# An mLSTM cell followed by a GELU block: the short rests of four pairs of hidden tiles in one TensorE section

## The chip, the cores and the metric

The kernel runs on one core of one Trainium2 chip. The metric is device time in microseconds (us) of one execution, the median of three runs. The engines are TensorE (PE in the profile, with its weight loads PEld), VectorE (DVE), ScalarE (ACT), GpSimd (POOL) and SyncE (SP), which issues most DMAs.

## The reference

An mLSTM cell runs over batch 4, 8 heads, 768 steps and head dimension 40. Its output, gated, is laid out as 3072 tokens of 320 values and goes through a two-layer block:

```
h = x @ w_in                               # x [3072, 320], w_in [320, 2048]
g = h * (1.0 / (1.0 + np.exp(-1.702 * h)))
return (g @ w_out).astype(np.float32)      # w_out [2048, 320]
```

Everything is fp32. The change concerns `x @ w_in`, the first product.

## The kernel before, in words

The 768 steps are cut into six blocks of 128 (w = 0 to 5; NW is 6). A block has 512 tokens: 128 steps of each of the 4 batches. For every block the first product is computed, then the second, and into the instructions of the second the cell of the next block is woven. The order on every engine is the order in which the instructions are written (`manual_schedule`, line 68); the framework inserts the waits and gives each new PSUM tile one of the banks of its pool.

**The first product.** The 2048 hidden columns are 8 pairs (j = 0 to 7) of two 128-column tiles. Block 0 is done plainly (`up`, line 614). Blocks 1 to 5 use `up_fast` (line 692): of the 320 input rows, the first 256 are a 2 by 2 scheme of 128-row parts and token halves, done with seven products of 128x128 by 128x256 instead of eight. The seven operands on the token side are sums made on VectorE in `token_sums` (line 673). The results of a pair are two rows of 512 tokens: row 0 (written to `g[:, 0]`) and row 1 (`g[:, 1]`). Product 1 is needed by itself, products 5 and 6 by themselves, products 2 and 3 add up in the bank of row 0, products 4 and 7 in that of row 1.

**The rests.** The last 64 of the 320 input rows are "the rest" of a row. A rest matmul has only 64 rows, so two of them, one for row 0 on partitions 0 to 63 and one for row 1 on partitions 64 to 127, run side by side in TensorE (line 717). They add into the same banks as products 2, 3, 4, 7. In an even pair they come last and in the odd pair after it first, so that those of two pairs stand together: four sections in a block, and twenty in blocks 1 to 5. In block 4 (`w == NW - 2`) each rest is cut into two halves of 256 tokens.

The profile records every fp32 matmul as two instructions, called passes here: the 280 calls of line 709 (5 blocks, 8 pairs, 7 products) are 560 records.

**The banks.** PSUM has eight banks. The pool `ps_m` (line 67) gives single banks, four of them; `ps_a` (line 66) gives two tiles of two banks. A pair takes two single banks (product 1; row 0) and one double tile `both` (row 1; products 5 and 6). A new tile has to wait until the last reader of an earlier tile in the same bank is done.

**Out of the banks.** After the matmuls of a pair ScalarE copies product 1 to `y` (line 743). VectorE adds product 6 to it (`u2`, line 746), then adds `u2` to product 5 and to the right half of row 1 in one instruction (line 747), and then makes `g[:, 1]` from row 1 (line 750). Row 0 is copied by ScalarE (line 754) and completed by GpSimd (line 755), but in pairs 6 and 7 VectorE does it in one instruction (line 757). The GELU of pair j-1 (`gelu_fast`, two ScalarE instructions, `g[:, 1]` first) stands in pair j between the copy of product 1 and that of row 0; that of pair 7 follows the loop (line 950).

**Beside it on VectorE.** Before pair 0, in blocks 1 to 4, VectorE does `token_sums` and then `gates(w + 1)` (lines 929 to 931), a chain of small instructions for the next block that ends in lines 325 and 326. After pairs 2 to 6 it does block transposes (`block_transposes`, line 394) for the next block: after pair 6 two of them, for n = 5 and 7 (line 942). Block 5 has no next block and none of this.

**The second product.** `down_fast` (line 805) follows at once. Each of its products runs over eight hidden tiles, two passes each. The first reads `g` of pairs 0 to 3, the second `g` of pairs 4 to 7 (line 810), so its seventh tile is `g[:, 0]` of pair 7.

Of the kernel before, what the change touches and what calls it, by code (L numbers as in the profile page):

```python
# [8 lines left out]
FP = mybir.dt.float32  # L9
# [3 lines left out]
OP = mybir.AluOpType  # L13
# [13 lines left out]
def kernel(  # L27
# [17 lines left out]
    NW = S // L  # L45
    NP = H // 2
    NF = DFF // 128
    D1 = D + 1
    DP = 64
    W = B * L  # L50
# [13 lines left out]
    op = ctx.enter_context(tc.tile_pool(name="op", bufs=2))  # L64
    rows = ctx.enter_context(tc.tile_pool(name="rows", bufs=2, space=bass.MemoryType.DRAM))
    ps_a = ctx.enter_context(tc.tile_pool(name="ps_a", bufs=2, space=PSUM))
    ps_m = ctx.enter_context(tc.tile_pool(name="ps_m", bufs=4, space=PSUM))
    ctx.enter_context(tc.manual_schedule())

    V, A, G, T = nc.vector, nc.scalar, nc.gpsimd, nc.tensor  # L70
# [15 lines left out]
    w_in_x = const.tile([128, NF // 2, 128], FP, name="w_in_x")  # L86
# [140 lines left out]
    kT, qT, ys, xT, gs, o_ps, sums, vw, x_row = {}, {}, {}, {}, {}, {}, {}, {}, {}  # L227
# [109 lines left out]
    def banks(name):  # L337
        return ps_a.tile([128, 2, 512], FP, tag="a", name=name)
# [322 lines left out]
    half_w = W // 2  # L661
    temps, second = {}, {}
# [25 lines left out]
    def gelu_fast(w, j):  # L688
        for i in (1, 0):
            A.activation(out=gs[w, j][:, i, :], in_=gs[w, j][:, i, :], func=AF.Gelu_apprx_sigmoid)  # L690

    def up_fast(w, j):

        x, rest_x = temps[w], xT[w].rearrange("p c b t -> p c (b t)")
        late = j % 2 == 0
        p1, row0 = (ps_m.tile([128, W], FP, tag="m", name="p_h") for _ in range(2))
        both = banks("p_h")  # L700
        row1 = both[:, 0, :]
        flat = both.rearrange("p i t -> p (i t)")
        left, right = slice(0, half_w), slice(half_w, W)
        f = lambda c, i: w_in_sb[:, c, (2 * j + i) * 128:(2 * j + i + 1) * 128]

        def product(n, out, start, stop):
            a = {1: lambda: f(0, 0), 2: lambda: f(1, 0), 3: lambda: s_in[:, 2, j], 4: lambda: f(1, 1),
                 5: lambda: s_in[:, 0, j], 6: lambda: s_in[:, 1, j], 7: lambda: f(0, 1)}[n]()
            T.matmul(out, a, x[n], start=start, stop=stop)  # L709

        def rest():
            n = 2 if w == NW - 2 else 1
            for h in range(n):
                t = slice(h * W // n, (h + 1) * W // n)
                for i, row in enumerate((row0, row1)):
                    r = slice(i * 64, i * 64 + 64)
                    T.matmul(row[:, t], w_in_x[r, j, :], rest_x[r, 2, t], start=(not late and h == 0),  # L717
                             stop=(late and h == n - 1))

        def row_0():  # L720
            product(2, row0[:, left], late, False)
            product(3, row0[:, right], False, not late)

        def row_1():
            product(4, row1[:, left], late, False)
            product(7, row1[:, right], False, not late)

        if not late:
            rest()
        product(1, p1[:, left], True, True)  # L730
        if late:
            row_0()
        product(5, both[:, 1, left], True, True)
        product(6, both[:, 1, right], True, True)
        row_1()
        if late:
            rest()
        else:
            row_0()
        y = work.tile([L, 2, DM + 64], FP, tag="y", name="parts").rearrange("p a b -> p (a b)")  # L740
        u2 = second[w]
        g = gs[w, j] = gp.tile([128, 2, W], FP, tag="g", name="g")
        A.copy(out=y[:, left], in_=p1[:, left])  # L743
        if j:
            gelu_fast(w, j - 1)
        V.tensor_tensor(out=u2, in0=both[:, 1, right], in1=y[:, left], op=OP.add)  # L746
        V.tensor_tensor(out=y[:, half_w:3 * half_w].rearrange("p (a t) -> p a t", a=2),  # L747
                        in0=flat[:, half_w:3 * half_w].rearrange("p (a t) -> p a t", a=2),
                        in1=u2.unsqueeze(1).to_broadcast([128, 2, half_w]), op=OP.add)
        V.tensor_tensor(out=g[:, 1, :], in0=row1, in1=y[:, half_w:3 * half_w], op=OP.add)  # L750
        u = y.rearrange("p (a t) -> p a t", t=half_w)[:, 0:3:2]
        g0 = g[:, 0, :].rearrange("p (a t) -> p a t", a=2)
        if j < NF // 2 - 2:
            A.copy(out=g[:, 0, :], in_=row0)  # L754
            G.tensor_tensor(out=g0, in0=g0, in1=u, op=OP.add)  # L755
        else:
            V.tensor_tensor(out=g0, in0=row0.rearrange("p (a t) -> p a t", a=2), in1=u, op=OP.add)
# [145 lines left out]
    for w in range(NW):  # L903
# [24 lines left out]
        else:  # L928
# [4 lines left out]
            for j in range(NF // 2):  # L933
                up_fast(w, j)
                if w == 1 and j < 4:
                    weight_sums(j)
                if more and j == 2:
                    load(w + 1, "vk")
                    columns_in(w + 1)
                    spread(w + 1)  # L940
                if more and j:
                    for n in ((), (0, 2), (4,), (6, 1), (3,), (5, 7), ())[j - 1]:
                        block_transposes(w + 1, n)
                if more and j == 7:
                    columns_turn(w + 1)
                if 2 <= j < 6:
                    hidden_difference(w, j - 2)
                if j >= 6:
                    hidden_sums(w, (j - 6,), G)
# [54 lines left out]
```

## Time and profile before

| | |
|---|---|
| median of 3 runs | 466.91 us (466.19 to 467.08) |
| the profiled execution | 466.95 us; its span in the trace 465.2 us |
| TensorE busy | 459.8 us, 99% of the span, 5063 matmul records |
| VectorE, ScalarE, GpSimd busy | 340.3, 189.5, 163.5 us |
| line 709, the seven products | 240 + 160 + 80 + 80 records, 66.9 + 41.1 + 23.9 + 23.8 us |
| line 717, the rests of blocks 1 to 5 | 128 records of 64x512 and 64 of 64x256, 31.8 + 8.0 us |
| block 2, first product | 182.5 to 215.0 us of the span |

Times in views of the trace are us from the start of the span, then the duration in us; a line of the timeline may merge several instructions (x4). Busy times of matmuls overlap, since a pass starts before the one ahead of it has left the array: what a pass costs is read from the distance of starts.

### The profile page before, as it was taken

The numbers are of one execution on the slowest core, as the hardware profiler recorded it, in microseconds if no ns is written. First come the engines' busy times: TensorE is split into PE (matmuls) and PEld (weight loads), VectorE is DVE, ScalarE is ACT, GpSimd is POOL, SyncE is SP. The second block draws the span as 40 slices with busy tenths as digits, with TensorE's granted clock in tenths as the row PEclk, the third lists the DMA queues.
The fourth block names the chain that finished last, engine by engine and source line by source line (L and its number), as shares of the span: only waits on it lengthen the run. The fifth ranks groups of instructions, "written<-read, shape, count | busy, mean of one in ns | idle before, by whom it ended". The sixth has DMA issues, their size and how long they took to land.

```text
span 465.2 us, 12360 instructions
## 1 busy us (share of the span) xinstructions
PE 459.8 (99%) x5063; PEld 387.8 (83%) x5063; DVE 340.3 (73%) x698; ACT 189.5 (41%) x433; POOL 163.5 (35%) x153
## 2 busy tenths in 40 slices
PE   8999999999999999999999999999999999999996
PEld 6877877776769999778999678999878999777996
DVE  5788999699779777688875688876768867535622
ACT  5686779001546500654700554900454810354100
POOL 5101318000898600365700266700248510157000
PEclk9999999999999999999999999999999999999999
DMA  8999998049993045996034988024999306000000
GB/s 165 186 306 234 242 220 179 3 105 188 143 153 97 18 98 122 182 140 132 3 72 126 193 133 156 12 58 99 195 140 106 90 19 140 28 1 0 1 29 30
DMA packets 135561, 52.87 MB, mean 114 GB/s; under 512 B 101984, under 2 KB 131632, under 8 KB 135504
## 3 DMA queue, kind: packets, MB, share of 16 engines
q1 hardware_dynamic: 127136, 50.27, 55.5%
q10 hardware_dynamic: 8048, 1.66, 1.8%
q8 instruction: 40, 0.66, 0.6%
q0 software_dynamic: 320, 0.15, 0.2%
q14 instruction: 17, 0.14, 0.1%
HBM read 44.52 MB, written 7.54 MB: 112 GB/s over the span
## 4 chain that ended last, share of the span: by engine, by line
PE 88%; POOL 4%; DMA 3%; DVE 2%; issue 1%; ACT 0%; SPq 0%; DVEq 0%; POOLq 0%
PE p_out L818 33%; PE p_h L709 21%; PE p_h L717 7%; PE p_h L626 6%; PE p_out L764 6%; PE p_c L602 3%; DMA q_sq<-in_q_dram 2%; PE p_o L503 2%; PE p_s L459 2%; PE p_i L511 2%; PE p_h L635 2%; PE p_t L386 1%; POOL g L755 1%; PE p_s L448 1%; POOL g L786 1%
## 5 line engine op out<-in xcount | busy, mean ns | idle before, releaser
L755 POOL TENSOR_TENSOR g<-g,parts 128x512 f32<-128x512 f32 x30 | 38.2, 1274 | 191.7 <-DVE parts L747 184.3
L743 ACT COPY parts<-p_h 128x256 f32<-128x256 f32 x40 | 14.9, 373 | 152.0 <-PE p_h L709 149.2
L818 PE MATMUL p_out<-w_out_sb,g 128*128 128x160 f32 x480 | 69.6, 301 | 0.1
L818 PEld LDWEIGHTS p_out<-w_out_sb,g 128*128 128x128 f32 x480 | 66.5, 190 | 1.2 <-ACT g L690 0.4
L709 PE MATMUL p_h<-xT,w_in_sb 128*128 128x256 f32 x240 | 66.9, 388 | 0.0
L690 ACT ACTIVATE g<-g 128x512 f32<-128x512 f32 x80 | 50.1, 631 | 40.0 <-DVE g L750 24.3
L709 PEld LDWEIGHTS p_h<-xT,w_in_sb 128*128 128x128 f32 x240 | 43.7, 190 | 18.5 <-issue 7.5
L823 DVE TENSOR_TENSOR o_sb<-o_sb,p_out 128x160 f32<-128x160 f32 x70 | 21.4, 317 | 41.0 <-PE p_out L818 40.4
L818 PE MATMUL p_out<-t_sb,s 128*128 128x160 f32 x320 | 47.1, 300 | 0.0
L746 DVE TENSOR_TENSOR t_x<-p_h,parts 128x256 f32<-128x256 f32 x40 | 16.7, 419 | 39.1 <-PE p_h L717 33.0
L818 PEld LDWEIGHTS p_out<-t_sb,s 128*128 128x128 f32 x320 | 44.4, 190 | 0.2
L709 PE MATMUL p_h<-t_x,s_in 128*128 128x256 f32 x160 | 41.1, 379 | 0.0
L717 PE MATMUL p_h<-xT,w_in_x 64*128 64x512 f32 (+1 forms) x192 | 39.8, 540 | 0.0
L435 ACT ACTIVATE wt<-wt,cols 128x64 f32<-128x64 f32 x160 | 38.8, 335 | 0.1
L764 PE MATMUL p_out<-w_out_sb,g 128*128 128x320 f32 x128 | 35.7, 436 | 0.0
L709 PEld LDWEIGHTS p_h<-t_x,s_in 128*128 128x128 f32 x160 | 30.4, 190 | 4.2
L764 PEld LDWEIGHTS p_out<-w_out_sb,g 128*128 128x128 f32 x128 | 23.9, 190 | 9.6
L747 DVE TENSOR_TENSOR parts<-p_h,t_x 128x512 f32<-128x512 f32 x40 | 27.7, 692 | 3.6
L754 ACT COPY g<-p_h 128x512 f32<-128x512 f32 x30 | 17.4, 580 | 30.4 <-PE p_h L717 25.1
L626 PE MATMUL p_h<-xT,w_in_sb 128*128 128x256 f32 x128 | 29.6, 384 | 0.0
L717 PEld LDWEIGHTS p_h<-xT,w_in_x 64*128 64x128 f32 x192 | 16.9, 186 | 14.7 <-issue 13.7
L750 DVE TENSOR_TENSOR g<-p_h,parts 128x512 f32<-128x512 f32 x40 | 27.6, 691 | 1.4
(203 smaller groups left out, 840.5 us busy)
## 6 DMA issues: line engine op xcount, KB each, us to landing
q_sq<-in_q_dram SPq DMA_DIRECT2D x20, 320.0 KB, 10.4
wt<-m_row SPq DMA_DIRECT2D x20, 256.0 KB, 5.8
k_sq<-in_k_dram SPq DMA_DIRECT2D x16, 320.0 KB, 6.4
out_dram<-o_sb SPq DMA_DIRECT2D x24, 160.0 KB, 2.0
eo<-in_o_gate_dram SPq DMA_DIRECT2D x5, 640.0 KB, 8.1
bits<-in_moe_w_in_dram SPq DMA_DIRECT2D x6, 512.0 KB, 9.6
q_sq<-x_row SPq DMA_DIRECT2D x10, 256.0 KB, 2.8
v_st<-in_v_dram SPq DMA_DIRECT2D x14, 160.0 KB, 5.2
```

The costliest lines, as they stand in the source:

```text
L435: A.activation(out=x[:, h, :], in_=x[:, h, :], func=AF.Exp, scale=-1.0, bias=cols[w][:, c * PH + h:c * PH + h + 1])
L626: T.matmul(ph[j][i][:, t], w_in_sb[:, c, f * 128:(f + 1) * 128], x[:, c, t], start=(first and c == 0 and n == 0), stop=(not first and c == ...
L690: A.activation(out=gs[w, j][:, i, :], in_=gs[w, j][:, i, :], func=AF.Gelu_apprx_sigmoid)
L709: T.matmul(out, a, x[n], start=start, stop=stop)
L717: T.matmul(row[:, t], w_in_x[r, j, :], rest_x[r, 2, t], start=(not late and h == 0), stop=(late and h == n - 1))
L747: V.tensor_tensor(out=y[:, half_w:3 * half_w].rearrange("p (a t) -> p a t", a=2), in0=flat[:, half_w:3 * half_w].rearrange("p (a t) -> p a ...
L750: V.tensor_tensor(out=g[:, 1, :], in0=row1, in1=y[:, half_w:3 * half_w], op=OP.add)
L754: A.copy(out=g[:, 0, :], in_=row0)
L755: G.tensor_tensor(out=g0, in0=g0, in1=u, op=OP.add)
L764: T.matmul(po, gs[w, f // 2][:, f % 2, b * L:(b + 1) * L], w_out_sb[:, f, :], start=(f == 0), stop=(f == NF - 1))
L818: T.matmul(po, a(f), b[:, f, :], start=(f == 0), stop=(f == NH - 1))
L823: V.tensor_tensor(out=dst, in0=x, in1=po, op=OP.add)
```

## The change

The rests of four pairs stand together. With k = j mod 4, the group's first pair (k = 0, so j = 0 and 4) does its products and its own rests, and then the rests of pairs j+2, j+3 and j+1, in this order. Pairs j+1, j+2, j+3 find their rests already in their banks and only add their products. So a block has two sections of rests instead of four, each twice as long.

The banks are shared out anew. Products 5 and 6 get a single bank `p56` of their own. In pair k = 0 all four tiles (product 1, `p56`, row 0, row 1) are single banks; the rows of k = 1 are two single banks that have to come free within the section; the rows of k = 2 and k = 3 are the two double tiles. The order of the products changes in pair k = 2: 4, 7, 2, 3, then 1, 5, 6. Before, it was 1, 2, 3, 5, 6, 4, 7 and the rests in even pairs. Odd pairs keep 1, 5, 6, 4, 7, 2, 3.

On VectorE the one instruction of line 747 becomes two of 256 tokens: product 5 plus `u2`, and the right half of row 1 plus `u2`. On ScalarE the copy of row 0 comes first in pair k = 2. The rests are cut into halves in block 4 as before, and also for pairs 0 and 1 of block 3.

```
+    def row_product(w, j, start):
+        n = 2 if w == NW - 2 or (w == NW - 3 and j < 2) else 1
+        for h in range(n):
+            t = slice(h * W // n, (h + 1) * W // n)
+            for i, row in enumerate(row_banks[w, j]):
+                r = slice(i * 64, i * 64 + 64)
+                T.matmul(row[:, t], w_in_x[r, j, :], xT[w][r, 2].rearrange("p b t -> p (b t)")[:, t],
+                         start=(start and h == 0), stop=(not start and h == n - 1))
+
+    def bank(name="p_h"):
+        return ps_m.tile([128, W], FP, tag="m", name=name)
...
-        late = j % 2 == 0
-        p1, row0 = (ps_m.tile([128, W], FP, tag="m", name="p_h") for _ in range(2))
-        both = banks("p_h")
-        row1 = both[:, 0, :]
...
-        if not late:
-            rest()
-        product(1, p1[:, left], True, True)
-        if late:
-            row_0()
-        product(5, both[:, 1, left], True, True)
-        product(6, both[:, 1, right], True, True)
-        row_1()
-        if late:
-            rest()
-        else:
-            row_0()
...
+        if k == 2:
+            row0, row1 = row_banks[w, j]
+            row_1()
+            row_0()
+        p1, p56 = bank(), bank()
+        if k == 0:
+            row0, row1 = row_banks[w, j] = bank(), bank()
+        elif k != 2:
+            row0, row1 = row_banks[w, j]
+        product(1, p1[:, left], True, True)
+        if k == 0:
+            row_0()
+        product(5, p56[:, left], True, True)
+        product(6, p56[:, right], True, True)
+        if k != 2:
+            row_1()
+        if k % 2:
+            row_0()
+        if k == 2:
+            copy_row()
         A.copy(out=y[:, left], in_=p1[:, left])
+        V.tensor_tensor(out=u2, in0=p56[:, right], in1=y[:, left], op=OP.add)
+        V.tensor_tensor(out=y[:, 2 * half_w:3 * half_w], in0=p56[:, left], in1=u2, op=OP.add)
+        if k == 0:
+            row_product(w, j, False)
+            for n in (2, 3):
+                both = banks("p_h")
+                row_banks[w, j + n] = both[:, 0, :], both[:, 1, :]
+                row_product(w, j + n, True)
+            row_banks[w, j + 1] = bank(), bank()
+            row_product(w, j + 1, True)
         if j:
             gelu_fast(w, j - 1)
-        V.tensor_tensor(out=u2, in0=both[:, 1, right], in1=y[:, left], op=OP.add)
-        V.tensor_tensor(out=y[:, half_w:3 * half_w].rearrange("p (a t) -> p a t", a=2),
-                        in0=flat[:, half_w:3 * half_w].rearrange("p (a t) -> p a t", a=2),
-                        in1=u2.unsqueeze(1).to_broadcast([128, 2, half_w]), op=OP.add)
+        V.tensor_tensor(out=y[:, half_w:2 * half_w], in0=row1[:, right], in1=u2, op=OP.add)
         V.tensor_tensor(out=g[:, 1, :], in0=row1, in1=y[:, half_w:3 * half_w], op=OP.add)
...
-        if j < NF // 2 - 2:
-            A.copy(out=g[:, 0, :], in_=row0)
+        if apart:
+            if k != 2:
+                copy_row()
             G.tensor_tensor(out=g0, in0=g0, in1=u, op=OP.add)
         else:
             V.tensor_tensor(out=g0, in0=row0.rearrange("p (a t) -> p a t", a=2), in1=u, op=OP.add)
```

Here `apart` is `j < NF // 2 - 2`, true for pairs 0 to 5, and `copy_row()` is ScalarE's copy of row 0 to `g[:, 0]`, left out where `apart` is false.

More of the change, by code (lines that the diff above doesn't have):

```diff
@@ L690, in gelu_fast @@
             A.activation(out=gs[w, j][:, i, :], in_=gs[w, j][:, i, :], func=AF.Gelu_apprx_sigmoid)
-    def up_fast(w, j):
-        x, rest_x = temps[w], xT[w].rearrange("p c b t -> p c (b t)")
-        late = j % 2 == 0
-        p1, row0 = (ps_m.tile([128, W], FP, tag="m", name="p_h") for _ in range(2))
-        both = banks("p_h")
-        row1 = both[:, 0, :]
-        flat = both.rearrange("p i t -> p (i t)")
+    row_banks = {}
+    def row_product(w, j, start):
[8 more added lines that the diff above has]
+        return ps_m.tile([128, W], FP, tag="m", name=name)
+    def up_fast(w, j):
+        x = temps[w]
+        k = j % 4
         left, right = slice(0, half_w), slice(half_w, W)
@@ L709, in product @@
             T.matmul(out, a, x[n], start=start, stop=stop)
[L711 to L718, printed above, removed]
         def row_0():
-            product(2, row0[:, left], late, False)
-            product(3, row0[:, right], False, not late)
+            product(2, row0[:, left], k == 0, False)
+            product(3, row0[:, right], False, k > 0)
         def row_1():
-            product(4, row1[:, left], late, False)
-            product(7, row1[:, right], False, not late)
-        if not late:
-            rest()
-        product(1, p1[:, left], True, True)
-        if late:
-            row_0()
-        product(5, both[:, 1, left], True, True)
-        product(6, both[:, 1, right], True, True)
-        row_1()
-        if late:
-            rest()
-        else:
-            row_0()
+            product(4, row1[:, left], k == 0, False)
+            product(7, row1[:, right], False, k > 0)
         y = work.tile([L, 2, DM + 64], FP, tag="y", name="parts").rearrange("p a b -> p (a b)")
@@ L742, in up_fast, with copy_row @@
         g = gs[w, j] = gp.tile([128, 2, W], FP, tag="g", name="g")
-        A.copy(out=y[:, left], in_=p1[:, left])
+        apart = j < NF // 2 - 2
+        def copy_row():
+            if apart:
+                A.copy(out=g[:, 0, :], in_=row0)
+        if k == 2:
[18 more added lines that the diff above has]
+            copy_row()
+        A.copy(out=y[:, left], in_=p1[:, left])
+        V.tensor_tensor(out=u2, in0=p56[:, right], in1=y[:, left], op=OP.add)
[8 more added lines that the diff above has]
+            row_product(w, j + 1, True)
         if j:
             gelu_fast(w, j - 1)
-        V.tensor_tensor(out=u2, in0=both[:, 1, right], in1=y[:, left], op=OP.add)
-        V.tensor_tensor(out=y[:, half_w:3 * half_w].rearrange("p (a t) -> p a t", a=2),
-                        in0=flat[:, half_w:3 * half_w].rearrange("p (a t) -> p a t", a=2),
-                        in1=u2.unsqueeze(1).to_broadcast([128, 2, half_w]), op=OP.add)
+        V.tensor_tensor(out=y[:, half_w:2 * half_w], in0=row1[:, right], in1=u2, op=OP.add)
         V.tensor_tensor(out=g[:, 1, :], in0=row1, in1=y[:, half_w:3 * half_w], op=OP.add)
@@ L752, in up_fast @@
         g0 = g[:, 0, :].rearrange("p (a t) -> p a t", a=2)
-        if j < NF // 2 - 2:
-            A.copy(out=g[:, 0, :], in_=row0)
+        if apart:
+            if k != 2:
+                copy_row()
             G.tensor_tensor(out=g0, in0=g0, in1=u, op=OP.add)
```

## The prediction

> **What bounds the kernel now.** I read four views in this order: the page's busy times, the chain of work that ended last, TensorE's timeline through a section of rests, and the timelines of VectorE and ScalarE at both ends of a block. The page first:
>
> ```profile
> PE 459.8 (99%) x5063; PEld 387.8 (83%) x5063; DVE 340.3 (73%) x698; ACT 189.5 (41%) x433; POOL 163.5 (35%) x153
> ...
> PEclk9999999999999999999999999999999999999999
> ```
>
> TensorE is busy 99% of the time at the full granted clock, so every gap of its own is time of the kernel. The chain through the first product of block 2 is TensorE alone:
>
> ```profile
> 182.53 3.02 PE p_h L709 x14
> 185.55 1.92 PE p_h L717 x8
> 187.47 6.24 PE p_h L709 x28
> ```
>
> Product pairs and sections of rests alternate, with no wait for another engine. What a section costs beyond its work is read from the starts in TensorE's timeline:
>
> ```profile
> 184.96 0.59 PE L709 MATMUL p_h<-xT,w_in_sb 128*128 128x256 f32 x2
> 185.48 1.99 PE L717 MATMUL p_h<-xT,w_in_x 64*128 64x512 f32 x8
> 187.40 0.70 PE L709 MATMUL p_h<-xT,w_in_sb 128*128 128x256 f32 x2
> 187.94 1.03 PE L709 MATMUL p_h<-t_x,s_in 128*128 128x256 f32 x4
> ...
> 193.12 0.59 PE L709 MATMUL p_h<-xT,w_in_sb 128*128 128x256 f32 x2
> ```
>
> From 187.94 to 193.12 there are 24 passes, 0.216 us each. In the weight loads inside the section two following steps start at 186.02 and 186.45: a double step (a pass of each row, side by side) takes 0.43. So the two passes from 184.96 should end at 185.39, and the section starts at 185.48, 0.09 late; its four double steps should take 1.72 and take 1.92 (185.48 to 187.40), 0.20 more; the two passes after it take 0.54 instead of 0.43, 0.11 more. One section costs 0.40 us for the change of shape. The step from one pair's rests to the next pair's inside it costs nothing.
>
> The head of the block, on VectorE:
>
> ```profile
> 188.11 0.14 DVE L326 TENSOR_TENSOR both<-m_run 32x1 f32<-32x1 f32 x1
> 188.18 0.41 DVE L746 TENSOR_TENSOR t_x<-p_h,parts 128x256 f32<-128x256 f32 x1
> 188.62 0.69 DVE L747 TENSOR_TENSOR parts<-p_h,t_x 128x512 f32<-128x512 f32 x1
> ```
>
> `u2` of pair 0 follows the last gate instruction without a gap: it is queued behind the gates, 2.70 us after the section has begun. Today nobody waits for it. The end of the block:
>
> ```profile
> 211.23 0.42 DVE L746 TENSOR_TENSOR t_x<-p_h,parts 128x256 f32<-128x256 f32 x1 [1.35 <-PE p_h L717]
> ...
> 213.69 2.06 DVE L394 STREAM_TRANSPOSE qT<-q_sq 128x512 f32<-128x512 f32 x2
> ...
> 215.00 4.64 PE L818 MATMUL p_out<-w_out_sb,g 128*128 128x160 f32 x32
> 215.59 0.41 DVE L746 TENSOR_TENSOR t_x<-p_h,parts 128x256 f32<-128x256 f32 x1
> ...
> 217.55 1.23 ACT L690 ACTIVATE g<-g 128x512 f32<-128x512 f32 x2 [3.12 <-DVE g L750]
> ```
>
> Pair 6's `u2` starts at 211.23, and from there VectorE works without a gap through two transposes to pair 7's `u2` at 215.59. Its last GELU ends at 217.55 + 1.23 = 218.78. The second product starts at 215.00 and reaches pair 7's row 0 with its 29th pass; a pass takes 0.136 (in block 5, without a wait, 12 passes lie between 431.14 and 432.77), so it is wanted at 215.00 + 28 x 0.136 = 218.81. There is no slack left. In block 1 TensorE already waits here:
>
> ```profile
> 146.80 0.57 PEld L818 LDWEIGHTS p_out<-w_out_sb,g 128*128 128x128 f32 x4 [0.39 <-ACT g L690]
> ```
>
> **The change part by part.** The sum is made against the profiled execution, 466.95 us with a span of 465.2; the median, 466.91, is 0.04 below it.
>
> *Sections.* Twenty become ten, each of eight double steps. TensorE keeps the same passes: 10 x 0.40 = -4.0 us, 0.8 per block. Two rows of the trace bear on one page of the Trainium skill here. The last pass before the section has a modelled end of 184.96 + 0.59 = 185.55, and the section starts at 185.48, before it. TensorEngine Tiling (Array Packing), section Tiling Modes, says that a change of tiling mode drains the engine. A full drain would cost the 0.16 by which a 0.38 pass outlasts its spacing, at both edges, beside the two slow first steps of 0.10; that estimate is 0.53 a section and -5.3 in all, and the sum below would end at 467.7 instead. I take the measured 0.40.
>
> *The head of blocks 1 to 4.* Pair 0 now fills all four single banks, and within the section the rows of pair 1 need two of them back, products 1 and 5 of pair 1 the other two. When they come free in block 2: product 1 when ScalarE has copied it, 183.04 + 0.37 = 183.41; row 0 when it is copied, 186.70 + 0.58 = 187.28; `p56` after `u2` (188.18) and the 256-token add that now follows it (dependent adds start 0.44 apart: 188.62, + 0.42 = 189.04); row 1 after its own two adds (an independent 256-token add starts 0.34 after the one ahead, as in the token sums at 183.26 and 183.60, a dependent one 0.44: 188.96, 189.40, + 0.69 = 190.1). TensorE wants them so: the rests of pairs 0, 2, 3, 1 start at 185.48, 186.44, 187.30, 188.16 (the first double step 0.10 long), product 1 of pair 1 at 189.12, its product 5 at 189.66 (two passes, 0.54). Which bank a tile gets is the framework's choice; I let the first freed be the first taken. Then the rows of pair 1 have theirs in time, product 1 too, and product 5 waits for row 1's: 190.1 + 0.05 - 189.66 = 0.5, and 0.10 for the restart (in block 1's wait above the pass after it came 0.24 later, not 0.136). That is 0.6. If instead the rows of pair 1 get the bank of `p56`, they start at 189.1 instead of 188.16: 0.93 + 0.1 = 1.0. If nothing waited it would be 0; a gain is excluded, since no matmul is taken away. I take 0.6, as row 0's bank is free 1.8 us before `p56`'s. `u2` stands 2.71, 2.70, 2.70 and 2.54 after the section's start in blocks 1 to 4 (115.89, 188.18, 260.21, 332.10 against 113.18, 185.48, 257.51, 329.55 or 329.56), so 3 x 0.6 + 0.44 = +2.2. Block 5 has no gates; its token sums end at 400.95, 0.7 us before its first section: 0. The second section of each block: VectorE there carries transposes, but by the same reckoning `p56` of pair 4 is free 4.7 us after the pair's start and wanted at 5.8: 0.
>
> *The end of blocks 1 to 4.* In pair 6 (k = 2) products 5 and 6 now come last, so `u2` cannot start before the pair's end. Call the start of pair 7 T. Before, `u2` started at 211.23 with T = 211.87, so T - 0.64. After: the last pass of product 6 starts at T - 0.22, lasts 0.38, and VectorE follows 0.15 later (as at 211.08 to 211.23): T + 0.3. The chain behind it stays as long: before, 4.36 from 211.23 to 215.59; after, 0.44 + 0.34 + 0.45 (two adds for one) + 0.61 + 0.60 + 0.96 + 0.94 = 4.34. So `u2` of pair 7 starts at T + 4.64. No section now stands ahead of pair 7, so its 14 passes take 3.02 and the second product starts at T + 3.02: `u2` is 1.62 behind that, where it was 0.59 (215.59 against 215.00). From `u2` to the end of the GELU it is 3.2 as before, and the 29th pass comes at 1.62 + 3.24 = 4.86 instead of the 3.81 it is wanted at: 1.06 + 0.10 of waiting, less the 0.13 it loses already (the seven passes from 218.40 take 1.25, and 6 x 0.136 + 0.30 would be 1.12) = 1.0. Blocks 3 and 4 have the same rows (287.63 and 359.72 for `u2`). In block 1, `u2` was 0.85 late and the wait 0.41; there 0.8 is added. Sum +3.8. Bounds: if the new adds start 0.1 further apart, in pairs 6 and 7, +0.2 a block (4.6); if the transposes did not stand in this chain, 0. In block 5 there are none: `u2` of pair 7 at T + 2.7, GELU in time, 0.
>
> *What is hidden.* The added 256-token add costs VectorE some 0.1 us a pair beside TensorE's 3.0; its share in the two chains is counted. Pair k = 2's earlier copy of row 0 frees GpSimd earlier, which has idle time in blocks 2 to 5. In block 1 GpSimd is full (weight sums of 2.9 us) and ScalarE queues behind it; pair 6's product 1 needs a bank by 138.2, and the bank of pair 5's product 1 is free by 136; if it had to be that of pair 5's row 0, copied at 138.29, it would cost 0.5. The half rests added in block 3 cost 0.01 (a section of halves takes 1.93). No DMA is moved.
>
> *Sum.* 466.95 - 4.0 + 2.2 + 3.8 = 469.0 us: about 0.45% slower. A change under 0.2% (0.9 us) could not be told from none.
>
> A rule that speaks against the change: TensorEngine Tiling (Array Packing), section Restrictions and Gotchas, says that row tiling raises PSUM pressure, as row tiles must write different banks. It has no price; taken as "every group waits for the slower bank choice", it would put 1.0 for each 0.6 above and end at 470.7.
>
> **The rivals.**
> 1. *The waits stay away* and only the saving counts: 466.95 - 4.0 = 463.0, faster. It needs `u2` of pair 0 to be 0.5 us earlier and that of pair 6 over 1 us earlier. For it: VectorE is 27% idle on average. Against: it has no gap in either chain above. It decides from the point where the two waits together fall below 0.8 us a block.
> 2. *Only the head waits* (the end of the block finds slack): 466.95 - 4.0 + 2.2 = 465.2, faster. Against it: block 1's wait for the GELU.
> 3. *The slower bank choice*, and adds 0.1 further apart: 466.95 - 4.0 + 3.9 + 4.6 = 471.5, slower.
> 4. *The saving does not come*, because the cost goes with the pairs and not with the sections: 469.0 + 4.0 = 473.0. Against it: inside a section the step between two pairs costs nothing.
>
> **How the numbers follow.** Forecast (468 to 470.3) 0.55, rival 3 with all between 0.2, rival 4 0.02; rival 2 0.1, rival 1 0.08, near no change 0.05. Faster 0.18, same 0.05, slower 0.77. The likeliest is 469.0. The range 465.2 to 471.5 leaves out rival 1, rival 4 and what lies beyond the ends.
>
> **What would show it.** Ten sections of 16 passes (more in blocks 3 and 4), 3.44 + 0.20 long. At the head of blocks 1 to 4 a wait of 0.5 us of TensorE for VectorE early in pair 1, or of 0.9 in the section. In pair 6 `u2` starting after pair 7's first pass. In blocks 1 to 4 a TensorE wait of about 1 us for ScalarE's line of the GELU, 3.7 us into the second product, and none in block 5, which should be 0.8 shorter. Wrong would be: no such waits, or a bank wait in pairs 2 to 5.

## The result and the profile after

The changed kernel takes 470.09 us (median of 4, 469.33 to 471.03) against 466.85 us for the kernel before: a ratio of 1.0073, 95% interval 1.0052 to 1.0094. It is slower by 0.7%, where 0.45% was forecast. The profiled execution is the fastest of the four, 469.33 us with a span of 467.6. Times here are medians and ratios are of means, and single runs of `a_pair6` (472.66 us), `a_turns` (476.61), `b_gates2` (472.87) and `b_turns` (476.80, left out of its numbers) were slower than the others of their kernel, at a mean granted clock of 0.988 to 0.993.

The page of the changed kernel: the engines' busy times and TensorE's granted clock.

```profile
PE 456.5 (98%) x5071; PEld 388.7 (83%) x5071; DVE 343.3 (73%) x738; ACT 186.0 (40%) x433; POOL 163.2 (35%) x153
...
PEclk9999999999999999999999999999999999999999
```

TensorE is busy 3.3 us less than before in a span 2.4 us longer: the sections cost less, and TensorE waits. The chain that ended last, through the first product of block 2 (start, duration, work):

```profile
188.45 0.07 DVE both L326
188.52 0.40 DVE t_x L762
188.94 0.42 DVE parts L763
189.36 0.34 DVE parts L774
189.73 0.70 DVE g L775
...
190.56 11.94 PE p_h L722 x54
202.50 3.63 PE p_h L701 x16
206.13 5.39 PE p_h L722 x24
```

Before, this stretch was TensorE alone. Now the chain comes from the gates on VectorE (line 326) through the four adds of pair 0 to TensorE. A section of four pairs takes 3.63, and eight double steps of 0.43 are 3.44. The wait itself, in TensorE's timeline behind that section:

```profile
189.41 0.70 PE L722 MATMUL p_h<-xT,w_in_sb 128*128 128x256 f32 x2
190.56 1.10 PE L722 MATMUL p_h<-t_x,s_in 128*128 128x256 f32 x4 [0.45 <-DVE g L775]
```

Product 1 of pair 1 starts at 189.41. Its product 5 would follow 0.54 later, at 189.95; it starts at 190.56, when VectorE has made `g[:, 1]` of pair 0 (line 775), and its second pass comes 0.08 late. At the end of the block (the timeline of all engines):

```profile
212.48 0.42 DVE L762 TENSOR_TENSOR t_x<-p_h,parts 128x256 f32<-128x256 f32 x1 [1.71 <-ACT g L690]
...
215.00 2.08 DVE L394 STREAM_TRANSPOSE qT<-q_sq 128x512 f32<-128x512 f32 x2
...
215.23 3.97 PE L844 MATMUL p_out<-w_out_sb,g 128*128 128x160 f32 x28
...
216.91 0.42 DVE L762 TENSOR_TENSOR t_x<-p_h,parts 128x256 f32<-128x256 f32 x1
...
218.95 1.23 ACT L690 ACTIVATE g<-g 128x512 f32<-128x512 f32 x2 [3.20 <-DVE g L775]
...
220.23 0.57 PEld L844 LDWEIGHTS p_out<-w_out_sb,g 128*128 128x128 f32 x4 [1.27 <-ACT g L690]
220.23 0.81 PE L844 MATMUL p_out<-w_out_sb,g 128*128 128x160 f32 x4 [1.03 <-ACT g L690]
```

Pair 6's `u2` starts at 212.48, behind the start of pair 7 at 212.21. (The view names ScalarE's GELU as what ended that wait, but `u2` doesn't read its result; product 6 ends at 212.38, 0.10 before.) Pair 7's `u2` starts 1.68 us into the second product; TensorE does 28 passes and then stands still until the GELU ends at 220.18. The idle time of the weight loads that the GELU ended, from block 1 on (us in total, times, longest):

```profile
PEld p_out L844 <- ACT g L690: 5.1, 4, 1.3
```

It is one such wait in each of blocks 1 to 4.

The table has the distance, in us, between the first matmul records of the stages: first product (from its first pass to the second product's) / second product (to the next block's first pass, in block 5 to the end of the span). It is read from the starts in each trace. The last rows are experiments that follow.

| kernel | block 1 | block 2 | block 3 | block 4 | block 5 |
|---|---|---|---|---|---|
| before | 32.80 / 39.67 | 32.63 / 39.39 | 32.63 / 39.41 | 32.67 / 39.40 | 32.63 / 34.09 |
| changed | 32.74 / 40.56 | 32.60 / 40.56 | 32.48 / 40.56 | 32.33 / 40.53 | 31.84 / 34.10 |
| `a_pair6` | 32.74 / 39.62 | 33.09 / 39.63 | 33.00 / 39.62 | 32.85 / 39.61 | 31.84 / 34.10 |
| `a_gates` | 34.59 / 40.56 | 31.88 / 40.56 | 31.88 / 40.56 | 31.93 / 40.57 | 31.84 / 34.10 |
| `a_both` | 34.60 / 39.72 | 32.38 / 39.63 | 32.40 / 39.63 | 32.42 / 39.61 | 31.84 / 34.09 |
| `b_early` | 32.80 / 39.78 | 32.63 / 39.78 | 32.63 / 39.60 | 32.67 / 39.25 | 32.63 / 34.10 |
| `a_early` | 32.91 / 40.21 | 32.75 / 39.43 | 32.66 / 39.43 | 32.50 / 39.25 | 31.84 / 34.10 |
| `a_early_gates` | 32.93 / 39.26 | 32.03 / 39.26 | 32.08 / 39.26 | 32.09 / 39.25 | 31.84 / 34.11 |

Against the kernel before, the first products give 1.37 us and the second products take 4.35; the stretch ahead of block 1, which the change doesn't touch, was 0.56 shorter in this execution. The sum, 2.4, is the difference of the spans; without that stretch it is 2.98, near the 3.24 of the medians.

### The profile page after: what moved, and what is told of

Read it like the earlier page. It is cut to its first block, busy times and chain, and to the rows that moved or that the text cites. A ratio compares the mean times of both kernels' runs of the same rounds, so it can differ in the third digit from the quotient of the medians.

```text
span 467.6 us, 12393 instructions
## 1 busy us (share of the span) xinstructions
PE 456.5 (98%) x5071; PEld 388.7 (83%) x5071; DVE 343.3 (73%) x738; ACT 186.0 (40%) x433; POOL 163.2 (35%) x153
## 4 chain that ended last, share of the span: by engine, by line
PE 80%; DVE 12%; DMA 2%; ACT 2%; issue 2%; SPq 1%; DVEq 0%
PE p_out L844 30%; PE p_h L722 20%; PE p_h L626 6%; PE p_out L790 6%; PE p_h L701 5%; PE p_c L602 3%; PE p_o L503 2%; PE p_s L459 2%; PE p_i L511 2%; DVE qT L394 2%; PE p_h L635 2%; ACT g L690 2%; DMA k_sq<-in_k_dram 2%; DVE g L775 1%; DVE parts L763 1%
## 5 line engine op out<-in xcount | busy, mean ns | idle before, releaser
L722 PE MATMUL p_h<-xT,w_in_sb 128*128 128x256 f32 x240 | 65.9, 383 | 0.0
L690 ACT ACTIVATE g<-g 128x512 f32<-128x512 f32 x80 | 47.8, 630 | 33.1 <-DVE g L775 26.8
L722 PEld LDWEIGHTS p_h<-xT,w_in_sb 128*128 128x128 f32 x240 | 44.6, 190 | 11.9 <-ACT g L739 2.3
L701 PE MATMUL p_h<-xT,w_in_x 64*128 64x512 f32 (+1 forms) x200 | 37.1, 514 | 0.0
L701 PEld LDWEIGHTS p_h<-xT,w_in_x 64*128 64x128 f32 x200 | 18.5, 186 | 14.9 <-issue 14.1
L626 PE MATMUL p_h<-xT,w_in_sb 128*128 128x256 f32 x128 | 29.6, 384 | 0.0
L626 PEld LDWEIGHTS p_h<-xT,w_in_sb 128*128 128x128 f32 x128 | 23.6, 190 | 5.3 <-issue 2.4
```

Source lines behind the costliest of these rows:

```text
L626: T.matmul(ph[j][i][:, t], w_in_sb[:, c, f * 128:(f + 1) * 128], x[:, c, t], start=(first and c == 0 and n == 0), stop=(not first and c == ...
L701: T.matmul(row[:, t], w_in_x[r, j, :], xT[w][r, 2].rearrange("p b t -> p (b t)")[:, t], start=(start and h == 0), stop=(not start and h == ...
```

## The experiments

The letter a stands for the changed kernel with an edit, b for the kernel before with one.

**The price of a section.** Every pair's rests stand behind its own products: forty sections. (Odd pairs thereby also take the product order of the even ones.)

```
-        late = j % 2 == 0
+        late = True
```

> The kernel before, with the rests of every pair behind its own products: eight sections of one pair in each block instead of four of two, forty in all instead of twenty. Theory: the price goes with the sections, 0.40 us each: 20 x 0.40 = +8.0 us, less the 0.85 us of waiting at the block ends, since pair 7's rests then stand between its products and the second product and give VectorE 1.3 us more: 466.9 + 7.1 = 474.0 us. Rival: the price goes with the rests themselves and not with the change of shape: 466 to 467 us.

Measured: 473.48 us, ratio 1.0144 (1.0123 to 1.0164), +6.65. The first products of blocks 2 to 5 take 34.12 to 34.16 us instead of 32.63 to 32.67: 1.49 for four sections, 0.37 each. The other end of the scale is block 5 of the changed kernel, where nothing waits: 0.79 less for two sections fewer, 0.40 each. The price goes with the sections.

**Pair 6 in the order of the odd pairs.**

```
-        if k == 2:
+        if j == 2:
             row0, row1 = row_banks[w, j]
             row_1()
             row_0()
...
-        if k != 2:
+        if j != 2:
             row_1()
-        if k % 2:
+        if k % 2 or j == 6:
             row_0()
```

> The changed kernel, but pair 6 does its products in the order of the odd pairs (1, 5, 6, then 4, 7, 2, 3); pair 2 keeps the new order. Theory: the wait at the end of blocks 1 to 4 (4 x 1.30 us in the trace of the changed kernel) comes from products 5 and 6 standing last in pair 6, so that VectorE starts pair 6's adds too late and the two transposes push pair 7's adds behind. With products 5 and 6 ahead, u2 of pair 6 starts about 1.7 us earlier, the last GELU ends 3.2 us into the second product instead of 5.0, it is wanted at 3.8, and all four waits go: 470.1 - 5.2 = 464.9 us. Rival: the end wait comes from the split of VectorE's one add into two, which lengthens its chain whatever the order: the waits stay, 470 us.

Measured: 467.41 us, ratio to the kernel before 1.0009 (0.9993 to 1.0025): 2.7 below the changed kernel, half of what was expected. The weight loads' wait for the GELU falls from 1.3 us a block to 0.3, so the order sets most of it, and the rival, the split add, falls as its main cause. But the first products of blocks 2 to 4 take about 0.5 us more than in the changed kernel. What the theory had missed comes out in `a_both`, below.

**The gates behind pair 0.**

```
-            if more:
-                gates(w + 1)
-                load(w + 1, "o")
             for j in range(NF // 2):
                 up_fast(w, j)
+                if more and j == 0:
+                    gates(w + 1)
+                    load(w + 1, "o")
```

> The changed kernel, but the gate chain of the next block is written behind pair 0 instead of ahead of it. Theory: the wait at the head (0.69, 0.69, 0.60 and 0.43 us in blocks 1 to 4) is there because pair 0's adds are queued behind the gates on VectorE; with the gates behind them the banks come free over 2 us earlier and the waits go: 470.1 - 2.4 = 467.7 us, the end waits unchanged at 1.3 each. Rival: the wait is one of banks as such, since pair 0 holds all four single banks until its rests are in and its rows are added, so that 0.5 us or so of it stays whatever VectorE does: 470 us.

Measured: 469.93 us, no gain in sum. The table tells why: in blocks 2 to 4 the head wait is gone (31.88, 31.88 and 31.93, as in block 5), which settles it against the banks as such; block 1 lost 1.85 us. VectorE there, and then GpSimd:

```profile
115.52 1.51 DVE L288 TENSOR_TENSOR_SCAN f_run<-one,fi 32x128 f32<-32x128 f32 x1
117.06 2.80 DVE L290 TENSOR_TENSOR st<-fi,f_run 32x128 f32<-32x128 f32 x1
```

```profile
115.49 1.26 POOL L781 TENSOR_TENSOR g<-g,parts 128x512 f32<-128x512 f32 x1 [34.06 <-ACT g L739]
116.72 3.01 POOL L803 TENSOR_TENSOR t_sb<-w_out_sb 128x1280 f32<-128x1280 f32 x1
```

Line 290 takes 0.28 us ahead of pair 0. Here it lasts until 119.86, just past the end of GpSimd's weight sum at 119.73, and the scan of line 288 until 117.03 beside GpSimd's instruction that ends at 116.75. So `u2` of pair 1 waits behind the gates until 122.48, and TensorE, idle for 1.1 us, for its bank. It is idle once more, for 0.9 us in pair 5, until ScalarE has copied an earlier row 0 (line 739).

**The same, with the weight sums one pair later.**

```
-                if w == 1 and j < 4:
-                    weight_sums(j)
+                if w == 1 and 1 <= j < 5:
+                    weight_sums(j - 1)
```

> The changed kernel with the gates behind pair 0 in all blocks, as in the second run of the first call, and GpSimd's four weight sums of block 1 one pair later. Theory: line 290 took 2.80 us there because it ran beside a weight sum of GpSimd; with none beside it, it takes 0.28 us again, and the wait of 1.23 us in pair 2 of block 1 goes. The weight sums come later and may be waited for elsewhere. Rival: line 290 is slow for another reason, the gates' place in the queue, and stays at 2 to 3 us.

One run, 468.96 us. VectorE in block 1:

```profile
114.81 1.51 DVE L288 TENSOR_TENSOR_SCAN f_run<-one,fi 32x128 f32<-32x128 f32 x1
116.36 0.28 DVE L290 TENSOR_TENSOR st<-fi,f_run 32x128 f32<-32x128 f32 x1
```

Line 290 is back at 0.28; the scan, which still has GpSimd's add (114.79 to 116.05) beside it, is still at 1.51. The first product of block 1 takes 32.18 us instead of 34.59. The later sums cost their own: the second product of block 1 takes 42.51. The collision is shown: line 290, a VectorE instruction with two SBUF inputs, did not finish until the GpSimd instruction that it ran beside did, and took its usual time without it, in the same place of the queue. The Trainium skill's GPSIMD Engine Reference, section Key points, says that GpSimd shares its SBUF interfaces with VectorE and that instructions with two SBUF inputs contend; the 2.80 against 0.28 agrees.

**Both edits together.**

> Both edits of the two runs before together: the gates behind pair 0 and pair 6 in the order 1, 5, 6, 4, 7, 2, 3. Theory: the two waits are independent and the full saving of the ten sections shows, with the 0.85 us that the kernel before waited at the ends as well: 470.1 - 5.2 - 2.4 = 462.5 us, 4.4 below the kernel before. Rivals: if the banks as such or the split adds set the waits, 465 to 470.

Measured: 467.56 us, ratio 1.0022 (1.0013 to 1.0032), 5 us above the theory. Block 1 has the collision just told. The rest is pair 6, in the timelines of TensorE's matmuls, VectorE and the weight loads in block 2:

```profile
209.47 0.59 PE L722 MATMUL p_h<-xT,w_in_sb 128*128 128x256 f32 x2
210.31 0.92 PE L722 MATMUL p_h<-t_x,s_in 128*128 128x256 f32 x3 [0.24 <-ACT g L739]
```

```profile
213.21 0.42 DVE L774 TENSOR_TENSOR parts<-p_h,t_x 128x256 f32<-128x256 f32 x1 [0.70 <-PE p_h L722]
```

```profile
220.09 0.57 PEld L844 LDWEIGHTS p_out<-w_out_sb,g 128*128 128x128 f32 x4 [0.34 <-ACT g L690]
```

With product 5 second in the pair, it comes 0.84 us after product 1 instead of 0.43: ScalarE has not yet copied row 0 of pair 5 out of the bank that it gets (line 739). The changed kernel's order, 4, 7, 2, 3 first, covers just that. And the end still waits 0.34, because pair 6's row 1 is now finished late, so that VectorE waits 0.70 inside its chain for products 4 and 7.

**The transposes behind pair 7**, and the same with the gates of blocks 2 to 4 behind pair 0.

```
-    for n in ((), (0, 2), (4,), (6, 1), (3,), (5, 7), ())[j - 1]:
+    for n in ((), (0, 2), (4,), (6, 1), (3,), (), (5, 7))[j - 1]:
```

> The changed kernel with the order of all products as it is, but the two block transposes that stand behind pair 6 on VectorE moved behind pair 7. Theory: the end wait is the sum of two things, u2 of pair 6 coming only after the pair's last product and 1.9 us of transposes between the adds of pairs 6 and 7. Without the transposes in between, u2 of pair 7 starts some 0.3 us before the second product and its last GELU ends about 3 us into it, wanted at 3.8: the four waits of 1.30 go and no matmul of pair 6 is disturbed (putting products 5 and 6 first cost a bank wait of 0.5 in pair 6 and left 0.36 at the end). 470.0 - 5.2 = 464.8 us. Rival: what VectorE does after the transposes, the sums for the third product of the second part, comes 2 us later and is waited for there: 466 to 468 us.

> The run before, and in blocks 2 to 4 the gate chain behind pair 0; block 1 keeps it ahead, since there the chain behind pair 0 ran into GpSimd's weight sums (line 290 took 2.80 us instead of 0.28) and cost 1.8 us. Theory: the head waits of blocks 2 to 4 go too (their first product took 31.9 us with the gates behind against 32.3 to 32.6): 464.8 - 1.7 = 463.1 us, 3.7 below the kernel before. Rival: the gates then push VectorE's later work into a new wait: 464 to 466 us.

Measured: 472.48 us, ratio 1.015 (1.0108 to 1.0192), and 473.26 us, ratio 1.0152 (1.0134 to 1.017). The first run's rival was right, and by more than it asked; the second run is above both its theory and its rival for the same reason. VectorE and GpSimd at the start of the second product of block 2, in `a_turns`:

```profile
222.85 2.34 DVE L820 TENSOR_TENSOR s<-g 128x512 f32<-128x512 f32 x2
225.11 2.92 DVE L823 TENSOR_TENSOR s<-s,g 128x512 f32<-128x512 f32 x2
```

```profile
223.29 3.04 POOL L588 TENSOR_TENSOR vw<-v_st,cols 128x656 f32<-128x656 f32 x2 [2.29 <-ACT cols L367]
226.30 2.32 POOL L579 TENSOR_TENSOR state_mid<-state,cols 128x328 f32<-128x328 f32 x2
```

The same two pairs of sums, and GpSimd, in the kernel before:

```profile
218.23 1.35 DVE L794 TENSOR_TENSOR s<-g 128x512 f32<-128x512 f32 x2
219.49 1.29 DVE L797 TENSOR_TENSOR s<-s,g 128x512 f32<-128x512 f32 x2
```

```profile
220.42 2.75 POOL L588 TENSOR_TENSOR vw<-v_st,cols 128x656 f32<-128x656 f32 x2 [4.53 <-ACT cols L367]
```

There all four had begun before GpSimd did; the last ran from 220.09 to 220.78, partly beside it, and took its usual 0.69. Behind the two transposes only the first begins before GpSimd, the other three are stretched, and TensorE waits for them and, further on, for the state. In the profiled execution, the slowest of the four, the clock then falls too; the other three, 472.18 to 472.58 us, had a mean granted clock of 1.0, so the median's loss is not the clock's. In `a_turns_gates` all four had 0.992 to 0.996. Stretches of block 1 in `a_turns`: us, TensorE busy and records, the same for its weight loads, VectorE, ScalarE and GpSimd, granted clock, DMA share, GB/s:

```profile
156.10:159.50 3.40, 2.04 (x89) 1.72 (x92) 3.30 (x7) 0.51 (x1) 1.84 (x2) 1.00 0.02 5
159.50:162.90 3.40, 3.40 (x65) 3.28 (x56) 2.90 (x5) 0.00 (x0) 0.00 (x0) 0.50 0.00 0
```

After a stretch in which TensorE was busy 60% of the time it ran 3.4 us at half clock. Nothing like it follows the changed kernel's own waits: the 3.4 us from 144.1, which hold its wait for the GELU in block 1, have TensorE busy for 2.37 us, 70%, and the clock stays at 1.00.

**The same move in the kernel before.**

> The kernel before with the two transposes moved behind pair 7 and nothing else. Theory: the end of blocks 1 to 4 already lost 0.41, 0.13, 0.15 and 0.15 us there; this goes: 466.8 - 0.8 = 466.0 us. Rival: what is moved is waited for in the second product: 467 us or more.

Measured: 470.31 us (468.09 to 472.54), ratio 1.008 (1.0048 to 1.0112). Not even the 0.8 us was gained; the rival again.

**The gates behind pair 0 in the kernel before**, blocks 2 to 4 alone.

> The kernel before with the gate chain of blocks 2 to 4 behind pair 0. Theory: in the kernel before nobody waits for pair 0's adds in time, because pair 1 has banks of its own; so the place of the gates makes no difference: 466.8 us. The head wait would then belong to the new sharing of the banks alone. Rival: the gates ahead of pair 0 cost something in any version: 465 to 466 us.

Measured: 466.55 us, ratio 1.0023 (0.9991 to 1.0055), and 32.66 us in the first products of blocks 2 and 3: the place of the gates makes no difference there. The head wait needs both, the gates ahead of pair 0 and the new sharing of the banks.

**The transposes earlier**, in the changed kernel and in the kernel before.

```
-    for n in ((), (0, 2), (4,), (6, 1), (3,), (5, 7), ())[j - 1]:
+    for n in ((), (0, 2), (4, 6), (1, 3), (5, 7), (), ())[j - 1]:
```

> The changed kernel with the block transposes one step earlier: (0, 2), (4, 6), (1, 3), (5, 7) behind pairs 2 to 5 and none behind pair 6 or 7. Moving them behind pair 7 only pushed VectorE's sums into GpSimd's work, where they were stretched. Theory: with none between the adds of pairs 6 and 7 the last GELU ends about 3 us into the second product, wanted at 3.8, and VectorE has room for the earlier transposes (it is behind pair 4's adds by 4.8 us and they are wanted at 5.8): the four waits of 1.30 go, 470.0 - 5.2 = 464.8 us. Rival: VectorE is then too late for the banks in pair 4 or 5 and TensorE waits there: 466 to 470 us.

> The kernel before with the earlier transposes of the two runs above. Theory: only the 0.84 us that its blocks 1 to 4 lose at the end go: 466.7 - 0.8 = 465.9 us, so that most of what the two runs above gain is the ten sections. Rival: if the transposes are what costs in any version, it comes down to 463 as well.

Measured: 465.56 us, ratio 0.9975 (0.9966 to 0.9985), for the changed kernel: 4.5 below it without the edit, and 1.2 below the kernel before. Its trace has no wait for the GELU any more, with the order of the products as it was: without the two transposes between the adds of pairs 6 and 7 the late `u2` of pair 6 costs nothing there. The second product of block 1 still takes 40.21: VectorE's sums are stretched beside GpSimd (two of them take 3.50 us from 146.97), and TensorE waits 0.7 us for the state. For the kernel before 467.17 us, ratio 1.001 (1.0001 to 1.002): the wait for the GELU is gone, but no time. VectorE and then TensorE in the second product of its block 2:

```profile
227.28 1.47 DVE L579 TENSOR_TENSOR state<-state_mid,cols 128x328 f32<-128x328 f32 x1
```

```profile
227.98 1.16 PE L459 MATMUL p_s<-qT,kT 40*64 40x64 f32 x64
229.43 1.05 PE L459 MATMUL p_s<-qT,kT 40*64 40x64 f32 x57 [0.29 <-DVE state L611]
```

Line 579, also with two SBUF inputs, takes 0.50 us in the kernel before:

```profile
227.34 0.50 DVE L579 TENSOR_TENSOR state<-state_mid,cols 128x328 f32<-128x328 f32 x1
```

Here GpSimd's mask (line 439, two instructions from 227.27 to 229.76) has moved beside it, and the scores wait for the state. So the earlier transposes are not a gain by themselves.

**The transposes earlier and the gates of blocks 2 to 4 behind pair 0.** Block 1 keeps its gates ahead:

```
-            if more:
+            if w == 1:
                 gates(w + 1)
                 load(w + 1, "o")
             for j in range(NF // 2):
                 up_fast(w, j)
+                if w > 1 and more and j == 0:
+                    gates(w + 1)
+                    load(w + 1, "o")
```

> The run before with the gate chain of blocks 2 to 4 behind pair 0. Theory: both waits go, save the head of block 1: 464.8 - 1.7 = 463.1 us, below the kernel before by 3.7. Rival: 464.8 or more, if the gates behind pair 0 now meet the earlier transposes.

Measured: 463.69 us, ratio to the kernel before 0.9939 (0.9926 to 0.9952). It is 3.1 us faster than the kernel before and 6.4 faster than the changed kernel, and the theory was 0.6 off. The chain of its block 2:

```profile
181.99 3.02 PE p_h L722 x14
185.01 3.63 PE p_h L701 x16
188.65 12.31 PE p_h L722 x56
200.96 3.80 PE p_h L701 x16
204.76 9.26 PE p_h L722 x42
214.02 8.69 PE p_out L844 x64
```

It is TensorE alone again, with two sections in place of four. The second section, 3.80 instead of 3.63, has a small wait; the head wait of block 1 is still there, since its gates stayed ahead. By the table, against the kernel before, 2.4 us come from the first products, the saving of the sections less the waits that are left, and 0.8 from the second products. The kernel before with both edits was not run; each of them alone gained nothing there.

## Why the prediction was right, step by step

*The sections.* -4.0 us was forecast, 0.40 for each of ten. Block 5 shows 0.79 for its two, `b_alone` 0.37 for each of twenty more. Right.

*The head of blocks 1 to 4.* +2.2 was forecast: 0.6 in blocks 1 to 3 and 0.44 in block 4, as a wait of product 5 of pair 1 for VectorE's last add of pair 0. The waits in the trace are 0.69, 0.69, 0.60 and 0.43 (the last as 0.32 of waiting and 0.10 for the restart), 2.4 in all. In block 2 the last add started at 189.73, where 189.40 was reckoned from a head that began 0.26 earlier; the bank choice, a guess in the forecast, was the first of the two that were priced. Blocks 2 to 4 of `a_gates` show that the gates cause it, and `b_gates2` that they did not matter with the old banks. The rest of what the first products did not give, about 0.2 us, is for the most part a wait in pair 4 that was priced at 0: its row 1 needs the bank of pair 3's products 5 and 6, and VectorE, behind two transposes, frees it too late, which costs 0.02 to 0.06 a block. The forecast had looked at the bank of pair 4's own products 5 and 6 alone. By its own list a bank wait in pairs 2 to 5 was a sign of being wrong; this one is there, but small.

*The end of blocks 1 to 4.* +3.8 was forecast, 1.0 in blocks 2 to 4 and 0.8 in block 1. Measured: 0.89 in block 1 and 1.17, 1.15 and 1.13 in blocks 2 to 4, sum 4.34. The mechanism is as told; the term was too small because `u2` of pair 7 started 1.68 into the second product and not 1.62, and its chain to the end of the GELU took 3.27 and not 3.2. The forecast let the new adds follow each other 0.34 and 0.44 apart; the first two of each pair stand 0.53 apart (212.48 and 213.01, 216.91 and 217.44). That could be read before: there line 747 followed line 746 in pair 6 after 0.53 too (211.23 and 211.76), and 0.44 was the spacing at the head of the block. `a_pair6` and `a_early` show the two parts of the mechanism, the late `u2` of pair 6 and the transposes behind it: 1.0 of the 1.3 goes with the one, all of it with the other.

*The sum.* 469.0 was forecast and 470.09 measured; of the 1.1 between them about 0.9 are these two terms, 0.55 at the ends and 0.4 at the heads, pair 4 included. The rest is within the 1.7 us by which the runs of the changed kernel differ.

*The rivals.* That the waits stay away fell with the trace, and so did the one that only the head waits. The slower bank choice did not come. The fourth, that the saving does not come, fell with block 5.

*Drain and banks.* The forecast's estimate for a full drain, from the Trainium skill's TensorEngine Tiling (Array Packing), section Tiling Modes, was 0.53 of a section; 0.37 to 0.40 was measured. The head wait, 0.43 to 0.69 a block, is a wait for a PSUM bank, the pressure that the section Restrictions and Gotchas of that page tells of, here because the rows of four pairs are in their banks at once.

## What to carry to other kernels

Where TensorE has no slack, as here, merging its sections can bring out waits for whoever empties its banks: follow each bank to its last reader, and ask what stands ahead of that reader in its own queue. A cheaper stage is worth having only when the side work is moved along with it: here the same ten sections cost 3 us or gave 3 us, depending on where the gates and the transposes stood on VectorE. Side work on VectorE must not be moved beside GpSimd without looking: an instruction with two SBUF inputs that began while GpSimd was at work ended only after GpSimd's.

## What the runs showed of the hardware

A VectorE instruction with two SBUF inputs (a scan, or a sum, difference or product) that begins while GpSimd is at work on a sum, a product or the mask ends only after it: line 290 took 2.80 instead of 0.28 us, the scan of line 288 1.51 instead of 0.41, line 579 1.47 instead of 0.50. In the fourteen traces, from block 1 on, none of 299 that began over 0.1 us after GpSimd's ended before it; of those that began closer together some were stretched and some not. One that begins first is not stretched: 0.69, as usual, for the sum that ran from 220.09 to 220.78 in the kernel before, beside GpSimd from 220.42. Adds with one input in PSUM ran beside the weight sums at their usual 0.42 (`a_gates`, 125.17 beside 124.71 to 127.63).

TensorE's granted clock went to half for 3.4 us in `a_turns` after 3.4 us in which it was 60% busy, though no single wait of its matmuls in them was longer than 1.04 us; passes then started 0.267 us apart instead of 0.136. Apart from the ends of the spans the kept traces have half clock in `a_turns` twice, in `a_turns_gates` twice, in `b_turns` twice and in `a_pair6` once, there ahead of block 1, where the edit changes nothing; TensorE was busy 49 to 63% of the 3.4 us ahead of each. After 70% in the changed kernel the clock stayed. That this share of busy time sets the clock, and where the limit lies, was not tested.
